# The last batch's second product in seven half-size products, and maxima that travel through DRAM

## The chip, the cores and the metric

The kernel runs on one core of one Trainium2 chip. The metric is the device time of one execution in microseconds (us). TensorE (PE) multiplies, VectorE (DVE) and ScalarE (ACT) do the elementwise work, GpSimd (POOL) almost nothing; SyncE (SP) issues nearly all DMAs, in the order of its queue.

## The reference

Sigmoid attention over 8 batches, 12 heads, 448 tokens, head size 64, and behind it two matrix products with a bend between them:

```python
scores = np.matmul(q, k.transpose(0, 1, 3, 2)) / np.sqrt(64) - np.log(448)
attn_out = np.matmul(1.0 / (1.0 + np.exp(-scores)), v)
x = attn_out.transpose(0, 2, 1, 3).reshape(8 * 448, 768)
h = x @ w_in                                # 768 x 2048
g = np.where(h >= 1, h, np.where(h <= -1, 0.0, (h + 1) ** 2 / 4.0))
out = g @ w_out                             # 2048 x 768
```

All inputs are float32.

## The kernel before

**Split operands.** From pair 8 on (a pair is two heads of one batch; 6 pairs a batch, 48 in all) every operand is scaled by a power of two and split into a high and a low float16 part, and each product of two matrices is three products (high by high, high by low, low by high). The scale comes from the largest magnitude of the operand. `prep_a` has ACT take the sums of magnitudes of q, k and v of a pair, per partition (`dump`, L597; from pair 47 on DVE takes maxima, L601). `all_sum` (L380) rounds these three columns to bfloat16 (`mb`, L383) and multiplies them by ones on PE, 128 x 3, so that every partition has the total; `total` (L664) puts this product into the score group of an earlier pair, in a spare part of its PSUM tile. `prep_b` (L604) makes the scales from it (L358 to L366, 3 columns each) and splits q, k and v (`hl`, `v`: ACT L627, DVE L628).

**A batch.** While the two big products of batch b run, the attention of batch b + 1 is spread between them: `scores` on PE, sigmoid and rounding on ACT (`psc` L736, `ahl` L744), the residue on DVE (`ahl` L745), `pav` on PE. Batch 7 has no attention of a next batch. The units of a batch are first the *ups* (x times w_in, with the bend), then the *downs* (g times w_out).

**The ups.** From batch 2 on `up_blocks` (L962) does 2 x 2 blocks in seven products instead of eight (`PRODUCTS`, L960): w_in in 8 sets i of prepared combinations, each product 128 x 128 by 224 columns, 9 of them a product, 63 an i, 504 a batch (`ph`). The sets were prepared in batch 1 by `mix` and `unmixed` and lie in DRAM (`blocks`); `load_set` brings them into three rotating slots. DVE adds the products up (L987, five of 224 columns an i; ACT L990, L996), and `bend` (L1021) does the bend on rows of 448, twice an i: ACT L1027, DVE L1028 and L1029, ACT's rounding L1030, DVE's residue L1031 into `ghl`, which holds all 16 chunks of g.

**The downs.** `down` (L1035) is plain: for 6 blocks m of rows of the output, 16 chunks by 3 products of 448 columns, 288 a batch (`po`), from `w_out_sb`, which holds all of w_out in both parts. DVE scales the result (L1064) and SP stores it. PSUM has three tiles (`ps_mo`) for `ph` and `po` together.

**The order.** `pin_order` (L282) plays the whole program with a list of costs (`Node.cost`): PE takes the first ready piece by rank, which is mostly the program's order; the other engines take, of what is ready, what is due first, where the due time comes from the PE products that need it (`play`, L226). The queues that come out are pinned. A DMA may not be placed earlier than 15 us ahead of its due time (L242).

Of the kernel before, what the change touches and what calls it, by code (L numbers as in the profile page):

```python
# [300 lines left out]
def sigmoid_attention_mlp(ctx: ExitStack, tc: tile.TileContext, first_qvk, qkv, w_in, w_out, out_t):  # L301
# [733 lines left out]
    def down(b, m, u, k):  # L1035
# [19 lines left out]
        if u == (hi - lo) // 2 - 1:  # L1055
# [8 lines left out]
                    nc.vector.tensor_scalar(out=o, in0=po[:, :S], scalar1=hold["od"], scalar2=None, op0=ALU.mult)  # L1064
# [126 lines left out]
    inv_x = finish_x(1)  # L1191
    common_scales(1, inv_x)
    mixed_at = plain_at = 0
    for b in range(1, B):
        units = ups_blocks(b) + downs(b)
        last = len(units) - 96 + LAST
        if b == 1:
# [76 lines left out]
```

## Time and profile before

| | |
|---|---|
| three runs | 1108.07, 1109.12, 1109.72 us; median 1109.12 |
| profiled execution | 1109.34 us |
| its span | 1107.6 us, 19890 instructions |
| busy | PE 1097.8, weight loads 671.8, DVE 896.6, ACT 783.8, POOL 1.3 us |
| granted clock | 1.00 |
| DMA | 151.63 MB, mean 137 GB/s |

How to read it: the span is from the first to the last instruction of one execution; the execution's own time has 1.74 us around it. In the busy lines "PEld" is PE's weight load, which overlaps products. A group row of the profile gives line, engine, operation, written tile <- read tiles, shapes and count, then busy us and mean ns of one, then the idle time of the engine just before these instructions and what ended it. A busy PE is not PE at its peak; what shows whether it was held up is what its instructions waited for.

### The profile page before, as it was taken

The numbers are of one execution on the slowest core, as the hardware profiler recorded it, in microseconds if no ns is written. First come the engines' busy times: TensorE is split into PE (matmuls) and PEld (weight loads), VectorE is DVE, ScalarE is ACT, GpSimd is POOL, SyncE is SP. The second block draws the span as 40 slices with busy tenths as digits, with TensorE's granted clock in tenths as the row PEclk, the third lists the DMA queues.
The fourth block names the chain that finished last, engine by engine and source line by source line (L and its number), as shares of the span: only waits on it lengthen the run. The fifth ranks groups of instructions, "written<-read, shape, count | busy, mean of one in ns | idle before, by whom it ended". The sixth has DMA issues, their size and how long they took to land.

```text
span 1107.6 us, 19890 instructions
## 1 busy us (share of the span) xinstructions
PE 1097.8 (99%) x7920; PEld 671.8 (61%) x7920; DVE 896.6 (81%) x1921; ACT 783.8 (71%) x1308; POOL 1.3 (0%) x8
## 2 busy tenths in 40 slices
PE   8999999999999999999999999999999999999998
PEld 2244445555447874588645885468844687459954
DVE  5999999989989997879957898679986799665820
ACT  6979998878966887568964789647886488533500
POOL 0000000000000000000000000000000000000000
PEclk9999999999999999999999999999999999999999
DMA  9924441242445605325161443416243151403400
GB/s 355 408 91 152 146 168 52 86 154 106 166 187 211 231 27 189 120 101 192 56 221 40 176 145 108 145 36 225 95 139 135 65 183 62 166 18 127 141 26 25
DMA packets 32222, 151.63 MB, mean 137 GB/s; under 512 B 3456, under 2 KB 14208, under 8 KB 25984
## 3 DMA queue, kind: packets, MB, share of 16 engines
q1 hardware_dynamic: 30400, 140.92, 35.5%
q10 hardware_dynamic: 1728, 9.44, 2.5%
q8 instruction: 62, 1.02, 0.4%
q14 instruction: 32, 0.26, 0.1%
HBM read 126.94 MB, written 23.40 MB: 136 GB/s over the span
## 4 chain that ended last, share of the span: by engine, by line
PE 90%; ACT 4%; DVE 3%; DMA 2%; issue 1%; ACTq 0%
PE po L425 38%; PE ph L425 34%; PE psc L425 10%; PE pav L425 9%; DMA w_out_sb<-w_in 1%; ACT a L733 1%; DMA blocks<-mixp 1%; DVE xhl L987 1%; DVE ahl L745 1%; ACT w_in_sb L498 1%; ACT mixp L945 0%; ACT ahl L744 0%; ACT psc L736 0%; DMA ghl<-first_qvk 0%; ACT mixs L930 0%
## 5 line engine op out<-in xcount | busy, mean ns | idle before, releaser
L425 PE MATMUL po<-ghl,w_out_sb 128*128 128x448 f16 x2304 | 445.2, 353 | 0.0
L425 PEld LDWEIGHTS <-w_in_sb 128*128 128x128 f16 x3708 | 353.2, 98 | 77.2 <-issue 18.0
L425 PEld LDWEIGHTS <-w_out_sb 128*128 128x128 f16 x2304 | 221.6, 98 | 216.6 <-issue 14.9
L425 PE MATMUL ph<-w_in_sb 128*128 128x224 f16 x3024 | 295.8, 259 | 0.3 <-DVE xhl L987 0.3
L745 DVE SCALAR_TENSOR_TENSOR ahl<-psc,ahl 128x896 f16<-128x896 f32 (+1 forms) x180 | 160.8, 901 | 63.6 <-ACT ahl L744 60.8
L736 ACT ACTIVATE psc<-psc,nls,sqk 128x896 f32<-128x896 f32 (+1 forms) x144 | 135.0, 966 | 72.4 <-PE psc L425 72.0
L744 ACT ACTIVATE ahl<-psc 128x896 f16<-128x896 f32 (+1 forms) x180 | 131.1, 760 | 9.8 <-DVE ahl L745 9.0
L425 PE MATMUL ph<-xhl,w_in_sb 128*128 128x448 f16 x576 | 111.6, 353 | 0.0
L987 DVE TENSOR_TENSOR xhl<-ph,xhl 128x224 f32<-128x224 f32 x240 | 88.9, 386 | 12.8 <-PE ph L425 7.6
L1030 ACT ACTIVATE ghl<-g 128x448 f16<-128x448 f32 x128 | 72.8, 575 | 32.8 <-DVE g L1029 32.1
L425 PE MATMUL psc<-hl 64*128 64x448 f16 (+1 forms) x744 | 85.0, 352 | 0.0
L1064 DVE TENSOR_SCALAR o<-po,od 128x448 f32<-128x448 f32 x42 | 28.6, 682 | 68.6 <-PE po L425 68.2
L1027 ACT ACTIVATE g<-xhl,hr,ihr 128x448 f32<-128x448 f32 x96 | 69.0, 756 | 21.1 <-DVE xhl L987 20.0
L1028 DVE SCALAR_TENSOR_TENSOR g<-g,rk 128x448 f32<-128x448 f32 x112 | 75.8, 681 | 7.8 <-ACT g L1027 7.3
L425 PE MATMUL pav<-ahl,v 128*64 128x448 f16 x792 | 81.8, 355 | 0.0
L1031 DVE TENSOR_TENSOR ghl<-g,ghl 128x448 f16<-128x448 f32 x128 | 77.9, 620 | 1.5
L627 ACT ACTIVATE hl<-raw,qkv_s 128x448 f16<-128x448 f32 x80 | 49.9, 664 | 24.8 <-DVE qkv_s L362 24.6
L1029 DVE SCALAR_TENSOR_TENSOR g<-xhl,ihs,g 128x448 f32<-128x448 f32 x96 | 64.9, 681 | 1.6
L597 ACT ACTIVATE dump<-raw 128x448 f16<-128x448 f32 (+1 forms) x107 | 63.5, 594 | 3.1 <-DMA raw<-qkv 1.9
L425 PEld LDWEIGHTS <-v 128*64 128x64 f16 x792 | 41.8, 110 | 37.9 <-issue 13.4
L628 DVE SCALAR_TENSOR_TENSOR hl<-raw,qkv_s,hl 128x448 f16<-128x448 f32 x80 | 52.2, 680 | 5.2 <-ACT hl L627 5.1
L425 PEld LDWEIGHTS <-hl 64*128 64x128 f16 (+1 forms) x744 | 29.5, 94 | 41.0 <-issue 19.2
(141 smaller groups left out, 898.9 us busy)
## 6 DMA issues: line engine op xcount, KB each, us to landing
w_in_sb<-blocks SPq DMA_DIRECT2D x48, 1344.0 KB, 6.1
raw<-qkv SPq DMA_DIRECT2D x36, 704.0 KB, 4.6
w_out_sb<-w_in SPq DMA_DIRECT2D x16, 768.0 KB, 11.7
out_t<-o SPq DMA_DIRECT2D x48, 224.0 KB, 2.1
blocks<-mixs SPq DMA_DIRECT2D x8, 768.0 KB, 3.8
w_out_sb<-w_out ACTq DMA_DIRECT2D x6, 768.0 KB, 5.3
raww<-w_out ACTq DMA_DIRECT2D x6, 768.0 KB, 4.5
blocks<-mixp SPq DMA_DIRECT2D x8, 576.0 KB, 4.7
```

The source lines that it names most:

```text
L425: ins = nc.tensor.matmul(*args, **kw)
L597: ins = nc.scalar.activation(dump[:, : rt.shape[1]], rt, AF.Abs, accum_out=m[:, t : t + 1])
L628: nc.vector.scalar_tensor_tensor(out=dst[:, 1, :], in0=rt, scalar=s[:, t : t + 1], in1=hi, op0=ALU.mult, op1=ALU.subtract)
L736: nc.scalar.activation(a, a, AF.Sigmoid, bias=nls, scale=sqk)
L744: nc.scalar.activation(hi, x, AF.Copy, scale=ATT)
L745: made.setdefault(i, []).append(nc.vector.scalar_tensor_tensor(out=lo, in0=x, scalar=ATT, in1=hi, op0=ALU.mult, op1=ALU.subtract))
L987: add = lambda out, q, other: nc.vector.tensor_tensor(out=out, in0=quarter(q), in1=other, op=ALU.add)
L1027: nc.scalar.activation(g, h, AF.Relu, bias=hr, scale=ihr)
L1028: nc.vector.scalar_tensor_tensor(out=g, in0=g, scalar=rt, in1=g, op0=ALU.min, op1=ALU.mult)
L1029: nc.vector.scalar_tensor_tensor(out=g, in0=h, scalar=ihs, in1=g, op0=ALU.mult, op1=ALU.max)
L1030: latest["g"] = nc.scalar.activation(hi, g, AF.Copy)
L1031: (nc.gpsimd if f % GPOOL else nc.vector).tensor_tensor(out=ghl[:, f, 1, :], in0=g, in1=hi, op=ALU.subtract)
```

## The change

**Downs of the last batch.** For batch 7 (`WB`) the plain downs give way to seven half-size products for 2 x 2 blocks, as in the ups: w_out's halves of chunks by halves of output rows, g's halves of chunks by halves of tokens. `down_blocks` does 21 turns (3 blocks m by 7 products), 8 chunks by 3 products of 224 columns each. The turns stand in the order `TURNS`: products 0 and 4 of all m, then 1, 2, 3, 6, 5 of each m; the first three turns are cut at chunk 5 (`STEPS`). ACT evicts products 0 and 4, DVE adds the others up; the last of all is one DVE addition of 224 columns and a store of 128 x 224.

**Combinations of g.** `bend_blocks` takes the place of `bend` in batch 7. Behind the same bend it makes four differences of 224 columns an i on DVE and splits seven parts instead of four: high and low of g's first halves (which products 0 and 4 need), and of the combinations (`gx`, three at a time as 672 columns, and the second half of chunk i). Its rows lie in a buffer of five (`gs`).

**Combinations of w_out.** `mix_out` and `unmixed_out`, eight of each, make the blocks and `send` stores them to DRAM (`out_blocks`, 56 stores). The program places them in batches 2 to 4, one each 13 units; their due times lie in batch 7. `load_unit` reads 21 units of 128 x 2048 into a ring of seven that lies where w_out lay: seven when the downs of batch 6 have read it, and one after each turn.

**Maxima.** From pair 20 on (`TOPS`) the three columns are written to DRAM and read back by all partitions (128 x 384, into an unused end of `w_out_sb`), both by SP, and DVE reduces them to three maxima in the scales' place; `mb` and its product are gone, 28 times.

**Planner.** A store to DRAM is no longer held to 15 us ahead of its due time.

The core of the diff:

```diff
-    ready = [x.due - 15e3 if x.dma and not x.fixed else 0.0 for x in nodes]
+    ready = [x.due - 15e3 if x.dma and not x.fixed and space(x.all[0].outs[0]) != "DRAM" else 0.0 for x in nodes]
...
             maxes[p] = m[:, :n]
+            if p >= TOPS:
+                nc.sync.dma_start(out=tops[p], in_=m)
+                nc.sync.dma_start(out=every, in_=tops[p].rearrange("k t -> (k t)").partition_broadcast(P))
...
-        m = sums.pop(p) if p in sums else alone(all_sum(m, n))
+        if p >= TOPS:
+            m = sml_p.tile([P, 3], F32, tag="m4", name="m4", bufs=1)
+            nc.vector.tensor_reduce(out=m, in_=every.rearrange("p (k t) -> p t k", t=3), axis=AX.X, op=ALU.max)
+        else:
+            m = sums.pop(p) if p in sums else alone(all_sum(m, n))
...
+    def mix_out(i):
...
+        for r, chunk in ((0, f), (1, g)):
+            nc.vector.tensor_tensor(
+                out=a[:, r], in0=w_out_sb[:, chunk, 0, :], in1=w_out_sb[:, chunk, 1, :], op=ALU.add
+            )
+        a11, a21, a12, a22 = a[:, 0, :H], a[:, 0, H:], a[:, 1, :H], a[:, 1, H:]
+        nc.vector.scalar_tensor_tensor(out=a22, in0=a21, scalar=ratio, in1=a22, op0=ALU.mult, op1=ALU.add)
+        nc.vector.tensor_tensor(out=a21, in0=a11, in1=a21, op=ALU.subtract)
+        nc.vector.scalar_tensor_tensor(out=a11, in0=a11, scalar=minus, in1=a22, op0=ALU.mult, op1=ALU.add)
+        nc.vector.tensor_tensor(out=a12, in0=a12, in1=a11, op=ALU.subtract)
...
+        for t in range(4):
+            send(i, 3 + t, sv[:, t].rearrange("p m h n -> p m (h n)"))
...
+    TURNS = [(m, j) for j in (0, 4) for m in range(HC)] + [(m, j) for m in range(HC) for j in (1, 2, 3, 6, 5)]
...
+    def bend_blocks(b, i):
...
+        parts(*(ghl[:, i + k, h, :].rearrange("p (t n) -> p t n", t=2) for h in range(2)), q[:, 2:4])
+        parts(ghl[:, i, 0, :HN], ghl[:, i, 1, :HN], q[:, 0])
+        for out, a, c in ((0, 1, 0), (1, 3, 1), (3, 3, 0), (2, 2, 3)):
+            nc.vector.tensor_tensor(out=q[:, out], in0=q[:, a], in1=q[:, c], op=ALU.subtract)
+        parts(ghl[:, i, 0, HN:], ghl[:, i, 1, HN:], q[:, 0])
+        parts(gx[:, i, :, 0], gx[:, i, :, 1], q[:, 1:4])
...
+    STEPS = [(u, 0, 5) for u in range(HC)] + [(u, 5, 8) for u in range(HC)]
+    STEPS += [(u, 0, 8) for u in range(HC, len(TURNS))]
...
+        for f in range(lo, hi):
+            for wh, gh in ((0, 0), (0, 1), (1, 0)):
+                mm(
+                    quarter(j), w[:, f, wh, :], part_of(f, gh), start=j in (0, 1, 2, 6) and f + wh + gh == 0,
+                    stop=f == k - 1 and wh == 1, skip_group_check=True,
+                )
+        if hi < k:
+            return
+        load_unit(n + NU)
...
+    turns = [60 + 13 * k for k in range(NFC)]
...
+                if b >= SB and (b - SB) * len(units) + u in turns:
+                    i = turns.index((b - SB) * len(units) + u)
+                    (mix_out, unmixed_out)[i % 2](i // 2)
```

On PE the order of products is the same up to the last batch but for the 28 that are gone and a few pieces of six `po` products that stand some pieces earlier. What moved on the other engines, at three places:

DVE at the end of the last batch's ups and behind them, before (the two L987 in one row are the last adds of the ups, for i = 7; g is the bend's row, L1031 the residue of 448):

```order
L1028 SCALAR_TENSOR_TENSOR g<-g,rk_11618 128x448
L1031 TENSOR_TENSOR ghl<-g,ghl 128x448
L1029 SCALAR_TENSOR_TENSOR g<-xhl,ihs_11622,g 128x448
L987 TENSOR_TENSOR xhl<-ph,xhl 128x224 x2
L1031 TENSOR_TENSOR ghl<-g,ghl 128x448
L1028 SCALAR_TENSOR_TENSOR g<-g,rk_11628 128x448
L1028 SCALAR_TENSOR_TENSOR g<-g,rk_11618 128x448
L1029 SCALAR_TENSOR_TENSOR g<-xhl,ihs_11632,g 128x448
L1029 SCALAR_TENSOR_TENSOR g<-xhl,ihs_11622,g 128x448
L1031 TENSOR_TENSOR ghl<-g,ghl 128x448 x2
L1064 TENSOR_SCALAR o<-po,od 128x448 x6
```

and now (L1083 are the adds, L1117 and L1118 the bend's steps, L1128 the differences, L1123 the residues; `w_out_sb` there is `gx`):

```order
L1083 TENSOR_TENSOR xhl<-ph,xhl 128x224 x2
L1128 TENSOR_TENSOR gs<-gs 128x224
L1123 TENSOR_TENSOR ghl<-gs,ghl 128x448
L1117 SCALAR_TENSOR_TENSOR g<-g,qm 128x448 x2
L1118 SCALAR_TENSOR_TENSOR gs<-xhl,ihs_11861,g 128x448 x2
L1123 TENSOR_TENSOR ghl<-gs,ghl 128x224
L1128 TENSOR_TENSOR gs<-gs 128x224
L1123 TENSOR_TENSOR ghl<-gs,ghl 128x448 x3
L1128 TENSOR_TENSOR gs<-gs 128x224 x15
L1123 TENSOR_TENSOR w_out_sb<-gs,w_out_sb 128x3x224 x5
L1123 TENSOR_TENSOR ghl<-gs,ghl 128x224 x5
L1235 SCALAR_TENSOR_TENSOR u<-po,od,u 128x224 x2
```

Seventeen differences and the combinations of five i stand behind the ups' last adds, ahead of the first sums of the downs; 15 differences, ten residues of 224 and three of 672 stand ahead of those adds, among the ups, where four residues of 448 stand now and thirteen stood before.

DVE in the downs of batch 4, between two attention pieces' residues (`ahl`), before:

```order
L793 TENSOR_REDUCE xm<-x_92 128x1 x2
L826 TENSOR_TENSOR xhl<-x_92 128x672
L383 CAST mb<-m_8063 128x3
L745 SCALAR_TENSOR_TENSOR ahl<-psc,ahl 64x448
L1064 TENSOR_SCALAR o<-po,od 128x448
L745 SCALAR_TENSOR_TENSOR ahl<-psc,ahl 128x896
L745 SCALAR_TENSOR_TENSOR ahl<-psc,ahl 64x448
L358 TENSOR_SCALAR qkv_e<-psc 128x3
```

and now:

```order
L805 TENSOR_REDUCE xm<-x_92 128x1
L1012 TENSOR_TENSOR omixa<-w_out_sb 128x768 x2
L1016 SCALAR_TENSOR_TENSOR omixa<-omixa,out_mixes 128x384
L757 SCALAR_TENSOR_TENSOR ahl<-psc,ahl 64x448
L1190 TENSOR_SCALAR o<-po,od 128x448
L757 SCALAR_TENSOR_TENSOR ahl<-psc,ahl 128x896
L757 SCALAR_TENSOR_TENSOR ahl<-psc,ahl 64x448
L619 TENSOR_REDUCE m_8277<-w_out_sb 128x3
```

The cast is gone, the reduction of 384 numbers (L619) stands ahead of the scales, and operations of `mix_out` stand between the pieces.

SP in the ups of batch 2, before (`blocks` are the sets of w_in, `raw` the pairs):

```order
L953 DMA w_in_sb<-blocks 128x5376 x2
L581 DMA raw<-qkv 128x1408
L953 DMA w_in_sb<-blocks 128x5376 x2
L1066 DMA out_t<-o 128x448
L581 DMA raw<-qkv 128x1408 x2
L1066 DMA out_t<-o 128x448
```

and now (`m` are a pair's columns):

```order
L965 DMA w_in_sb<-blocks 128x5376 x2
L609 DMA tops<-m_4027 128x3
L610 DMA w_out_sb<-tops 128x384
L609 DMA tops<-m_4381 128x3
L610 DMA w_out_sb<-tops 128x384
L586 DMA raw<-qkv 128x1408 x2
L1192 DMA out_t<-o 128x448
```

Writes and broadcasts of the maxima stand between the loads, in one queue with them.

More of the change, by code (lines that the diff above doesn't have):

```diff
@@ L54 @@
 SB = 2
+TOPS = 20
+WB = 7
 GROUPED = 8
@@ L555, in slot_of @@
         return (p + 2) % NFB
+    tops = drm_p.tile([NPAIR, P, 3], F32, name="tops")
+    every = w_out_sb.rearrange("p f h n -> p (f h n)")[:, -1024:-256].bitcast(F32)
     done = set()
@@ new lines, in block_scales, with out_scales, put @@
+        down_sc[b, None] = lambda: od
+    UNIT, NU = NFC // 2 * 2 * P, 7
+    wflat = w_out_sb.rearrange("p f h n -> p (f h n)")
+    ring = [wflat[:, k * UNIT : (k + 1) * UNIT] for k in range(NU)]
+    gx = wflat[:, NU * UNIT : NU * UNIT + NFC // 2 * 6 * HN].rearrange("p (f t h n) -> p f t h n", t=3, h=2, n=HN)
+    out_blocks = drm_p.tile([HC, 7, P, UNIT], F16, name="out_blocks")
+    out_mixed = {}
+    out_mixes = const.tile([P, 6], F32, name="out_mixes")
+    def out_scales():
+        def put(tag, in0, s1, op0, s2=None, op1=None):
+            out_mixed[tag] = t = out_mixes[:, len(out_mixed) : len(out_mixed) + 1]
+            nc.vector.tensor_scalar(out=t, in0=in0, scalar1=s1, scalar2=s2, op0=op0, **({"op1": op1} if op1 else {}))
+            return t
+        low = put("low", wo.scale[0], wo.scale[1], ALU.min, 0.25, ALU.mult)
+        put("inv", wo.inv[0], wo.inv[1], ALU.max, 4.0, ALU.mult)
+        put("to0", low, wo.inv[0], ALU.mult)
+        put("to1", low, wo.inv[1], ALU.mult)
+        put("ratio", wo.scale[1], wo.inv[0], ALU.mult)
+        put("minus", out_mixed["ratio"], -1.0, ALU.mult)
@@ new lines, in unmixed_out @@
+    def unmixed_out(i):
+        pl = raw_p.tile([P, 2 * DM], I32, tag="raww", name="omixp").bitcast(F16)[:, : 3 * DM]
+        pv = pl.rearrange("p (t m h n) -> p t m h n", t=3, m=HC, h=2)
+        for h in range(2):
+            f = w_out_sb[:, i, h, : DM // 2].rearrange("p (m n) -> p m n", m=HC)
+            nc.scalar.activation(pv[:, 0, :, h, :], f, AF.Copy, scale=out_mixed["to0"])
+            g = w_out_sb[:, i + NFC // 2, h, :].rearrange("p (t m n) -> p t m n", t=2, m=HC)
+            nc.scalar.activation(pv[:, 1:3, :, h, :], g, AF.Copy, scale=out_mixed["to1"])
+        for t in range(3):
+            send(i, t, pv[:, t].rearrange("p m h n -> p m (h n)"))
@@ L1066, in down, with down_blocks, part_of, quarter @@
             nc.sync.dma_start(out=dst, in_=o)
+    STEPS = [(u, 0, 5) for u in range(HC)] + [(u, 5, 8) for u in range(HC)]
+    STEPS += [(u, 0, 8) for u in range(HC, len(TURNS))]
+    def down_blocks(b, u, lo, hi):
+        cut()
+        m, j = TURNS[u]
+        n, k = (b - WB) * len(TURNS) + u, NFC // 2
+        if u == 0 and lo == 0:
+            hold["od"] = down_sc[b, None]()
+        if j == 0 and lo == 0:
+            hold["u", m] = tmp_p.tile([P, S], F32, tag="tmp", name="u")
+        if j in (0, 1, 2, 6) and lo == 0:
+            hold["q", m, j] = ps_mo.tile([P, 512], F32, tag="mo", name="po")
+        wt, xt, _ = PRODUCTS[j]
+        def part_of(f, gh):
+            return (
+                ghl[:, f, gh, :HN], ghl[:, f + k, gh, :HN], ghl[:, f + k, gh, HN:], ghl[:, f, gh, HN:],
+                gx[:, f, 2, gh], gx[:, f, 0, gh], gx[:, f, 1, gh],
+            )[xt]
+        home = {0: (0, 0), 4: (0, 0), 1: (1, 0), 2: (2, 0), 3: (2, 1), 5: (2, 0), 6: (6, 0)}
+        def quarter(j):
+            at, half = home[j]
+            return hold["q", m, at][:, half * 256 : half * 256 + HN]
+        w = ring[n % NU].rearrange("p (f h n) -> p f h n", f=k, h=2)
+        for f in range(lo, hi):
[3 more added lines that the diff above has]
+                    stop=f == k - 1 and wh == 1, skip_group_check=True,
+                )
+        if hi < k:
+            return
+        load_unit(n + NU)
+        od, u2, u3 = hold["od"], hold["u", m][:, :HN], hold["u", m][:, HN:]
+        def add(out, j, other):
+            nc.vector.scalar_tensor_tensor(out=out, in0=quarter(j), scalar=od, in1=other, op0=ALU.mult, op1=ALU.add)
+        def put(half, lo, hi, o):
+            row = (m + half * HC) * P
+            nc.sync.dma_start(out=out_t[row : row + P, b * S + lo : b * S + hi], in_=o)
+        if j == 0:
+            nc.scalar.activation(u2, quarter(0), AF.Copy, scale=od)
+        elif j == 4:
+            o = out_p.tile([P, S], F32, tag="o", name="o")[:, :HN]
+            nc.scalar.activation(o, quarter(4), AF.Copy, scale=od)
+            put(0, 0, HN, o)
+        elif j == 1:
+            add(u2, 1, u2)
+        elif j == 3:
+            add(u3, 2, u2)
+            hold["og"] = out_p.tile([P, S], F32, tag="o", name="o")
+            add(hold["og"][:, HN:], 3, u3)
+            put(1, HN, S, hold["og"][:, HN:])
+            add(u3, 3, u2)
+        elif j == 6:
+            o = out_p.tile([P, S], F32, tag="o", name="o")[:, :HN]
+            add(o, 6, u3)
+            put(0, HN, S, o)
+        elif j == 5:
+            add(hold["og"][:, :HN], 5, u2)
+            put(1, 0, HN, hold["og"][:, :HN])
@@ L1196, in sigmoid_attention_mlp @@
         last = len(units) - 96 + LAST
+        if b >= WB:
+            units = ups_blocks(b) + [lambda s=s: down_blocks(b, *s) for s in STEPS]
+            last = len(units) - (96 - LAST) // 2
+        if b == WB:
+            for n in range(NU):
+                load_unit(n)
+        if b == SB:
+            out_scales()
         if b == 1:
@@ L1204, in sigmoid_attention_mlp @@
         slow = [*range(n), *range(2 * n, 3 * n)] if b < SB else range(len(PRODUCTS) * NFC // 2)
-        share = [DW // 2 if u in slow else DW for u in range(last)]
+        share = [DW // 2 if u in slow else DW * (1 + (b >= WB)) for u in range(last)]
         share = [sum(share[:u]) / sum(share) for u in range(last + 1)]
```

51 lines of the change are left out of this document (48 added, 3 removed).

## The prediction

> **What bounds the kernel now.** I read the page's busy times first, then TensorE's waits, then busy times by stage, then the chain of waits in the last batch. The page:
>
> ```profile
> span 1107.6 us, 19890 instructions
> PE 1097.8 (99%) x7920; PEld 671.8 (61%) x7920; DVE 896.6 (81%) x1921; ACT 783.8 (71%) x1308; POOL 1.3 (0%) x8
> ```
>
> TensorE (PE) is busy 1097.8 of 1107.6 us. A busy matmul row could hide stalls, so here is what PE waited for; the largest and the only one on VectorE (DVE) in a batch:
>
> ```profile
> PE psc L425 <- DMA ghl<-first_qvk: 4.3, 1, 4.3
> PE ph L425 <- DVE xhl L987: 0.3, 1, 0.3
> ```
>
> So after the first load nothing makes PE wait, and the time is the sum of its products. Next, the stages (columns: PE, weight load, DVE, ACT, POOL busy, granted clock, DMA share, GB/s): one steady batch, its first half (ups) alone, and the last batch's ups and downs:
>
> ```profile
> 474.90:607.10 132.20, 132.20 (x1058) 89.13 (x1058) 108.66 (x245) 96.90 (x170) 0.00 (x0) 1.00 0.37 128
> 474.90:540.00 65.10, 65.10 (x645) 55.88 (x645) 59.41 (x127) 53.15 (x100) 0.00 (x0) 1.00 0.37 133
> 1001.20:1050.60 49.40, 49.40 (x511) 48.85 (x510) 38.63 (x80) 22.48 (x44) 0.00 (x0) 1.00 0.43 150
> 1050.60:1107.60 57.00, 53.52 (x284) 27.51 (x282) 9.08 (x15) 3.09 (x5) 0.00 (x0) 1.00 0.07 25
> ```
>
> PE has no gap at full granted clock. DVE, the fullest of the others, has 18% free over a batch, 9% in its ups and nearly everything in the last downs. A change can win by shortening PE's products, and lose where new DVE work makes PE wait.
>
> The chain that ends the kernel (start us, us, what):
>
> ```profile
> 1001.34 46.58 PE ph L425 x486
> 1047.91 1.14 PE po L425 x6
> 1049.05 1.72 PE ph L425 x18
> 1050.77 53.36 PE po L425 x282
> 1104.13 0.03 issue
> 1104.16 0.68 DVE o L1064
> ```
>
> **The change part by part.** *Products of the last down.* Before: 288 of 448 columns at 53.36 / 282 = 0.1892 us, 54.49 us. After: 21 turns of 24, so 504 of 224 columns. The ups stream exactly this size, at 46.58 / 486 = 0.0958 us: 48.30 us. Gain 6.19 us. Each of these has a weight load of 128 columns of its own, and the third window shows that stream just holding (48.85 of 49.40 us): no more is to be had.
>
> The Trainium skill, "TensorE: Matmul & The Clock Gate", section "Back-to-back issue gap", speaks against halving: for streams of weight load and matmul it gives 81 ns at 128 columns and 131 ns at 512. My estimate between these is 94 ns at 224 and 123 ns at 448, by which the down would grow from 35.3 to 47.1 us. The trace disagrees: 189 ns at 448 columns, and halves at 96.
>
> *The tail.* After the last product one DVE operation of 448 columns (0.68 us) becomes one of 224; the adds of 224 take 0.39 (rows below). Gain 0.27 us (0.39 is without a scalar operand: 0.2 to 0.3). The last store is half as large; I count nothing for it (0 to 0.3).
>
> *The maxima's products.* 28 products of 3 columns go. What one costs is read from two score groups that differ by it alone, x10 with and x9 without:
>
> ```profile
> 937.89 1.25 PE psc L425 x10
> 954.14 1.24 PE psc L425 x9
> ```
>
> 0.01 us: it lies in the change of tile shape between full and half tiles. 28 x 0.01 = 0.3 at most, by rounding perhaps 0; I take 0.14.
>
> *The last batch on DVE.* The groups of the last 106 us, and of the whole run, by mean ns:
>
> ```profile
> L987 DVE TENSOR_TENSOR xhl<-ph,xhl 128x224 f32<-128x224 f32 x40 | 14.9, 388 | 6.1 <-PE ph L425 3.0 <-ACT xhl L990 2.8
> L1028 DVE SCALAR_TENSOR_TENSOR g<-g,rk 128x448 f32<-128x448 f32 x16 | 10.9, 682 | 4.1 <-ACT g L1027 4.0
> L1031 DVE TENSOR_TENSOR ghl<-g,ghl 128x448 f16<-128x448 f32 x16 | 9.9, 622 | 0.7
> L826 DVE TENSOR_TENSOR xhl<-x 128x672 f32<-128x672 f32 x6 | 5.1, 849 | 0.0
> ```
>
> One round of i in the ups is these rows, from one L1028 with its wait to the next:
>
> ```profile
> 1028.53 0.68 DVE L1028 SCALAR_TENSOR_TENSOR g<-g,rk 128x448 f32<-128x448 f32 x1 [0.59 <-ACT g L1027]
> ...
> 1034.57 0.69 DVE L1028 SCALAR_TENSOR_TENSOR g<-g,rk 128x448 f32<-128x448 f32 x1 [0.59 <-ACT g L1027]
> ```
>
> 6.04 us, of which 0.59 idle: 5.45 us for 5 adds, 4 two-operand steps and 2 residues, whose means sum to 5.90. Neighbours overlap, so I price by 0.92 of the mean: 0.36 (224), 0.63 (step), 0.57 (448), 0.78 (672). The order of the new kernel says where the new work stands. Up to the last add of the ups it has 15 differences and 10 residues of 224, 3 residues of 672 and one step more than before, 9 residues of 448 fewer: 25 x 0.36 + 3 x 0.78 + 0.63 - 9 x 0.57 = 6.8 us. The waits of L1028 (4.0 us) are what DVE has spare; so it ends 2.8 us late. PE feels less: between the last read of a PSUM tile and the reuse of its buffer lie two products, 18 x 0.0958 = 1.7 us, less two adds (0.78) and handovers: about 0.7 us is forgiven. Stall 2.1.
>
> Then the downs. The last adds and ACT's read-out of 224:
>
> ```profile
> 1050.81 0.69 DVE L987 TENSOR_TENSOR xhl<-ph,xhl 128x224 f32<-128x224 f32 x2 [0.30 <-PE ph L425]
> L990 ACT ACTIVATE xhl<-ph 128x224 f32<-128x224 f32 x8 | 2.9, 357 | 25.1 <-PE ph L425 25.1
> ```
>
> Products 0 of the three m, cut at chunk 5, give 45 + 6 products, 4.9 us, before chunk 7 is needed. After the last add (0.7 us after the last up product) DVE has one difference, one residue, four steps, one short residue: 0.36 + 0.57 + 2.52 + 0.36 = 3.8; with 0.36 for ACT's rounding, 0.2 for handovers and the 0.7, 5.1. Stall 0.2. From there PE has 3 + 18 products, three turns 4 and seven eighths of turn (0, 1): 114 x 0.0958 = 10.9 us; DVE has 1 + 15 differences, 3 residues of 448 and 5 of 672 until the last combination is there: 16 x 0.36 + 3 x 0.57 + 5 x 0.78 = 11.4. Stall 0.5. Together 2.8 us. Ends: with differences at 0.31 the ups fit and it is 0.8; with full means about 5. Later turns find all in place; turns 0 and 4 are evicted by ACT, which had 22.48 of 49.40 us busy.
>
> *Loads of w_out blocks.* 7 units of 512 KB in the ups, 14 in the downs at one per turn of 2.3 us, each issued six turns (14 us) ahead. Rows of such transfers:
>
> ```profile
> w_in_sb<-blocks SPq DMA_DIRECT2D x48, 1344.0 KB, 6.1
> out_t<-o SPq DMA_DIRECT2D x48, 224.0 KB, 2.1
> o<-part SPq DMA_DIRECT2D x6, 224.0 KB, 2.7
> ```
>
> 1344 KB land in 6.1 us, so 512 KB in about 3: hidden behind 14. In the ups 3.7 MB join 150 GB/s x 49 us = 7.3 MB; together 224 GB/s, where the page's line of 40 slices begins with 408:
>
> ```profile
> GB/s 355 408 91 152 146 168 52 86 154 106 166 187 211 231 27 189 120 101 192 56 221 40 176 145 108 145 36 225 95 139 135 65 183 62 166 18 127 141 26 25
> ```
>
> Cost 0; if a set came late, its lateness.
>
> *Preparing the blocks (batches 2 to 6).* Eight times on DVE 2 sums of 768, 4 steps of 384, one residue of 768 and two of 384; on ACT three roundings of a mix and four copies of the unmixed parts. Rows of the like:
>
> ```profile
> L917 DVE TENSOR_TENSOR mixa<-w_in_sb 128x768 f32<-128x768 f16 x16 | 14.8, 952 | 0.0
> L922 DVE SCALAR_TENSOR_TENSOR mixa<-mixa,mixes 128x384 f32<-128x384 f32 x8 | 4.9, 618 | 0.2
> L931 DVE SCALAR_TENSOR_TENSOR mixs<-mixa,mixes,mixs 128x768 f16<-128x768 f32 x16 | 15.7, 1013 | 1.2 <-ACT mixs L930 1.2
> L930 ACT ACTIVATE mixs<-mixa,mixes 128x768 f16<-128x768 f32 x16 | 14.4, 931 | 8.8 <-DMA blocks<-mixp 6.6 <-DVE mixa L924 1.2 <-DVE mixa L922 1.0
> L793 DVE TENSOR_REDUCE xm<-x 128x1 f32<-128x448 f32 x48 | 28.8, 612 | 8.4 <-ACT x L792 7.7 <-ACT x L789 0.6
> L414 DVE TENSOR_REDUCE xm<-psc 128x1 f32<-128x128 f32 x6 | 1.7, 291 | 2.2 <-PE psc L425 2.1
> L383 DVE CAST mb<-m 128x3 bf16<-128x3 f32 (+1 forms) x40 | 6.7, 168 | 7.8 <-PE psc L425 5.8 <-ACT dump L597 1.8
> ```
>
> DVE: 2 x 0.95 + 6 x 0.62 + 1.01 = 6.6 us each. The new maximum over 384 numbers lies between 0.29 (128) and 0.61 (448): 0.55, less the cast of 0.17, 0.38 for each of 6 pairs. A batch with two mixes gains 13.2 + 2.3 = 15.5 us: 108.66 + 15.5 = 124 of 132.2, 94%. That is a little more than its ups hold today (91%) with no PE wait, and the order puts most of it into the downs. What it costs PE is not in the trace: 0 from that row, up to 5 if each of the 24 operations of about 1 us holds back a product by 0.2. I take 0.7, near the row. ACT gains at most 2 x 5 us a batch on 96.90. The planner's new rule for stores to DRAM lets them stand earlier; ACT's waits for `blocks<-mixp` in L930's row (6.6 us) may shrink, but PE did not wait for them: 0.
>
> *Maxima through DRAM.* The write and the broadcast take about 2.1 + 2.7 us plus two issues, in place of a product that waited for its score group. The two score groups above belong to neighbouring pairs, 16 us apart, and the operands of pair p + 2 are due about that much later; the reduction heads DVE's queue only where the order set it. Cost 0 in the forecast, priced as a rival.
>
> **The sum** against the profiled execution, 1109.34 us (span 1107.6 and 1.74 around it): -6.19 - 0.27 - 0.14 + 2.8 + 0.7 = -3.1, so 1106.2; the median of the runs, 1109.12, is 0.2 lower: **1106.0**.
>
> **Rivals.**
> *DVE eats the gain.* If DVE runs at full means and the mixes cost 2 us: -6.6 + 5 + 2, 1109.5: no change that can be told (0.2%, 2.2 us, is about what a measurement of this kernel tells). For it: the ups leave DVE 0.59 of 6.04 us. Against: the order keeps residues and differences behind the adds.
> *The reduction waits in DVE's queue (slower).* Behind it stand the score residues and the adds that PE needs. DVE has 132.2 - 124 = 8 us a batch left, 1.4 a pair. If the reduction waits longer than that for its broadcast, because SP is held by a load in front of it or the 1344 KB of a set (6.1 us) pass first, PE slips by the excess: at 1.7 us, 0.3 x 28 = 8.4, less the 3.1: 1114.4. For it: two hops of over 2 us where there was a product. Against: the pair of slack.
> *Halving costs.* If products from w_out went no faster than 0.108 us, 504 of them would take the old 54.5 us, and with the other terms it would be 1112. The ups' 0.0958 speak against it. The Trainium skill's rule above would put the kernel here or beyond.
> *All hidden.* No stall: 1109.1 - 6.6 = 1102.5.
>
> **Chances.** Forecast 0.60 (1102.6 to 1108), DVE eats the gain 0.18, reduction 0.11, halving 0.02, all hidden 0.09. The forecast holds a small part that rounds to no change, so: faster 0.63, same 0.23, slower 0.14. The range leaves out the reduction, halving and part of all hidden: 1102.5 to 1110.5.
>
> **What would show it.** Right: 504 products `po` of 224 columns at 0.096 us; PE waits for DVE of 2 to 4 us between the last third of the last ups and turn (0, 1), with DVE full there; elsewhere PE waits under 1.5 us; the same span of a score group without its product. Wrong: DVE idle before the reduction on a DMA by over 1 us a pair; PE waiting on `w_out_sb` from DRAM; the batches of 132.2 us growing by more than 1.

## The result, and the profile after

| | median us | lowest to highest | runs |
|---|---|---|---|
| before | 1108.62 | 1108.07 to 1109.72 | 4 |
| changed | 1119.22 | 1118.48 to 1119.67 | 4 |

The changed kernel is slower: ratio 1.0094, 95% interval 1.0076 to 1.0111. The forecast was 1106.0 us, 1102.5 to 1110.5.

The profiled execution took 1119.67 us. Its page begins:

```profile
span 1118.0 us, 20730 instructions
PE 1098.5 (98%) x8108; PEld 692.1 (62%) x8108; DVE 976.5 (87%) x2052; ACT 831.5 (74%) x1386; POOL 1.3 (0%) x8
```

PE is about as busy as before, although its products have become fewer columns, and the span is 10.4 us longer. The busy times by stage (columns as in the prediction's windows) show where. Before, batch 4 (3 and 5 have the same length), batch 6 and the last:

```profile
607.04:739.28 132.24, 132.24 (x1059) 89.17 (x1058) 108.69 (x245) 96.95 (x170) 0.00 (x0) 1.00 0.37 128
...
871.52:1001.18 129.66, 129.66 (x1036) 87.97 (x1035) 100.15 (x219) 82.01 (x135) 0.00 (x0) 1.00 0.29 102
1001.18:1107.60 106.42, 102.94 (x793) 76.38 (x791) 47.71 (x95) 25.57 (x48) 0.00 (x0) 1.00 0.23 83
```

And after, batches 4 to 7:

```profile
610.32:748.28 137.96, 134.44 (x1054) 89.73 (x1052) 123.31 (x264) 106.58 (x184) 0.00 (x0) 0.99 0.50 151
748.28:885.18 136.90, 134.22 (x1054) 89.53 (x1052) 123.52 (x264) 106.73 (x184) 0.00 (x0) 0.99 0.50 152
885.18:1016.85 131.67, 129.96 (x1032) 87.68 (x1031) 105.14 (x214) 86.06 (x141) 0.00 (x0) 1.00 0.39 125
1016.85:1118.00 101.15, 97.08 (x1009) 96.50 (x1007) 67.13 (x155) 34.33 (x70) 0.00 (x0) 1.00 0.55 189
```

Batch 4 starts 3.3 us later (610.32 against 607.04); batches 4, 5 and 6 grow by 5.7, 4.7 and 2.0, and the last takes 5.3 less: +10.4 together. So the half-size products bring most of what they were to bring, and 15.7 us are lost in the batches ahead of them. What PE waited for (us in total, times, longest):

```profile
PE ph L427 <- DVE xhl L1083: 6.3, 3, 2.5
...
PE psc L427 <- DVE ahl L757: 2.2, 2, 2.0
PE psc L427 <- DVE diag L403: 1.6, 2, 1.0
PE po L427 <- ACT ghl L1122: 0.5, 1, 0.5
```

Before, PE waited for DVE 0.5 us for `diag` (at 317.71, in batch 1, which the prediction's list leaves out) and 0.3 us for the adds. Now the adds of the ups (L1083) let PE wait 6.3 us in three places. The places in PE's timeline (start, us, instruction, idle time before it):

```profile
309.29 2.14 PE L427 MATMUL psc<-hl 64*128 64x448 f16 x12 [1.97 <-DVE ahl L757]
...
639.46 7.86 PE L427 MATMUL ph<-w_in_sb 128*128 128x224 f16 x63 [2.50 <-DVE xhl L1083]
...
776.97 7.86 PE L427 MATMUL ph<-w_in_sb 128*128 128x224 f16 x63 [2.06 <-DVE xhl L1083]
...
913.52 6.36 PE L427 MATMUL ph<-w_in_sb 128*128 128x224 f16 x63 [1.71 <-DVE xhl L1083]
```

One wait for the adds stands in the ups of each of batches 4, 5 and 6. The one at 309.29, in batch 1, is for `ahl`, and it comes before the first broadcast is issued (337.14), so no reduction that waits can be its cause. What DVE did ahead of the one at 639.46, with SP's queue beside it:

```profile
628.01 0.32 SPq L609 DMA_DIRECT2D tops<-m  x1
628.42 0.38 SPq L965 DMA_DIRECT2D w_in_sb<-blocks  x1
...
631.54 0.32 SPq L610 DMA_DIRECT2D w_out_sb<-tops  x1
...
638.16 0.66 DVE L619 TENSOR_REDUCE m<-w_out_sb 128x3 f32<-128x384 f32 x1 [3.17 <-DMA w_out_sb<-tops]
638.73 0.68 DVE L1083 TENSOR_TENSOR xhl<-ph,xhl 128x224 f32<-128x224 f32 x2
```

The write of the columns goes at 628.01, a set of 1344 KB right behind it, and the broadcast at 631.54, when the write has landed. The reduction stands at the head of DVE's queue and idles there for 3.17 us, until the broadcast is in at 638.16, 6.6 us after its issue. Behind it are two adds that PE needs, the 2.50 us above. DVE's waits of this kind over the whole run, and how long the two hops, broadcast and write, took to land (count, size, median us):

```profile
DVE m L619 <- DMA w_out_sb<-tops: 14.3, 8, 3.2
```

```profile
w_out_sb<-tops SPq DMA_DIRECT2D x28, 192.0 KB, 4.8
...
tops<-m SPq DMA_DIRECT2D x28, 1.5 KB, 4.0
```

Eight of 28 reductions found DVE waiting, 14.3 us in all, longest 3.2. The write takes 4.0 us and the broadcast 4.8 at the median, not 2.1 and 2.7.

The waits of PE are not the whole loss. The granted clock (the column ahead of the DMA share) in five us from one us behind each of the four waits above:

```profile
310.29:315.29 5.00, 5.00 (x33) 2.14 (x30) 3.73 (x9) 4.94 (x9) 0.00 (x0) 0.71 0.29 118
640.46:645.46 5.00, 5.00 (x38) 4.35 (x36) 4.39 (x8) 4.66 (x9) 0.00 (x0) 0.66 0.64 227
777.97:782.97 5.00, 5.00 (x40) 4.48 (x39) 4.39 (x8) 4.68 (x9) 0.00 (x0) 0.72 0.59 232
914.52:919.52 5.00, 5.00 (x53) 4.84 (x51) 4.83 (x10) 4.77 (x10) 0.00 (x0) 1.00 0.55 180
```

After three of the four PE ran below full clock; 5 us at 0.71, 0.66 and 0.72 cost 1.5, 1.7 and 1.4 us. That is how 63 products of one set took 7.86 us there and 6.36 behind the wait at 913.52: PE counts as busy and is slow. The waits for DVE in the rows above (6.3 + 2.2 + 1.6, 10.1 us, where before had 0.8) and the lower clock (4.6) come to 13.9 of the 15.7 us of this execution; 3.4 of them are the wait in batch 1 and the clock behind it.

The last batch's chain, from its first up product to the last addition:

```profile
1017.01 46.58 PE ph L427 x486
...
1071.17 43.49 PE po L427 x452
...
1114.69 0.45 DVE o L1235
```

The ups take 46.58 us as before, so DVE's new work there delays nothing, and the products of 224 columns run at 43.49 / 452 = 0.0962 us.

### The profile page after: what moved, and what is told of

The parts are those of the page before. It is cut to its first block, busy times and chain, and to the rows that moved or that the text cites. A ratio compares the mean times of both kernels' runs of the same rounds, so it can differ in the third digit from the quotient of the medians.

```text
span 1118.0 us, 20730 instructions
## 1 busy us (share of the span) xinstructions
PE 1098.5 (98%) x8108; PEld 692.1 (62%) x8108; DVE 976.5 (87%) x2052; ACT 831.5 (74%) x1386; POOL 1.3 (0%) x8
## 4 chain that ended last, share of the span: by engine, by line
PE 41%; DVE 29%; ACT 19%; DMA 6%; issue 5%; SPq 0%; ACTq 0%; DVEq 0%
PE po L427 20%; PE ph L427 12%; PE psc L427 5%; DVE ahl L757 5%; PE pav L427 5%; DMA w_out_sb<-tops 3%; DVE g L1154 3%; DVE xhl L1083 3%; DVE g L1155 3%; ACT dump L602 3%; ACT psc L748 2%; ACT ahl L756 2%; DVE ghl L1157 2%; ACT g L1153 2%; ACT hl L639 2%
## 5 line engine op out<-in xcount | busy, mean ns | idle before, releaser
L427 PE MATMUL po<-ghl,w_out_sb 128*128 128x448 f16 (+1 forms) x2304 | 419.2, 341 | 0.7 <-ACT ghl L1122 0.5
L427 PEld LDWEIGHTS <-w_out_sb 128*128 128x128 f16 x2520 | 241.9, 98 | 191.5 <-issue 16.0
L427 PE MATMUL ph<-w_in_sb 128*128 128x224 f16 x3024 | 299.3, 261 | 6.3 <-DVE xhl L1083 6.3
L1083 DVE TENSOR_TENSOR xhl<-ph,xhl 128x224 f32<-128x224 f32 x240 | 89.1, 386 | 11.5 <-PE ph L427 5.4
L1156 ACT ACTIVATE ghl<-g 128x448 f16<-128x448 f32 x112 | 63.2, 575 | 33.1 <-DVE g L1155 32.5
L1153 ACT ACTIVATE g<-xhl,hr,ihr 128x448 f32<-128x448 f32 x80 | 58.3, 756 | 25.4 <-DVE xhl L1083 25.0
L1154 DVE SCALAR_TENSOR_TENSOR g<-g,rk 128x448 f32<-128x448 f32 x96 | 65.0, 680 | 3.5 <-ACT g L1153 2.6
L1157 DVE TENSOR_TENSOR ghl<-g,ghl 128x448 f16<-128x448 f32 x112 | 67.4, 618 | 0.3
L427 PEld LDWEIGHTS <-v 128*64 128x64 f16 x792 | 42.1, 110 | 38.8 <-issue 14.6
L1155 DVE SCALAR_TENSOR_TENSOR g<-xhl,ihs,g 128x448 f32<-128x448 f32 x80 | 54.0, 681 | 1.4
L639 ACT ACTIVATE v<-raw,qkv_s 128x512 f16<-128x512 f32 x36 | 25.8, 717 | 27.3 <-DVE qkv_s L364 27.1
```

What stands on the lines that cost most here:

```text
L427: ins = nc.tensor.matmul(*args, **kw)
L639: nc.scalar.activation(hi, rt, AF.Copy, scale=s[:, t : t + 1])
L1083: add = lambda out, q, other: nc.vector.tensor_tensor(out=out, in0=quarter(q), in1=other, op=ALU.add)
L1153: nc.scalar.activation(g, h, AF.Relu, bias=hr, scale=ihr)
L1154: nc.vector.scalar_tensor_tensor(out=g, in0=g, scalar=rt, in1=g, op0=ALU.min, op1=ALU.mult)
L1155: nc.vector.scalar_tensor_tensor(out=g, in0=h, scalar=ihs, in1=g, op0=ALU.mult, op1=ALU.max)
```

## The experiments

Two theories stood at the start. One, *the round trip*: the reduction is set so early in DVE's queue that its broadcast has not landed, and DVE's queue behind it, then PE, pay for that. The rival, *DVE is full*: the preparation of the w_out blocks takes DVE's spare time in batches 2 to 6 and makes its adds late, whatever the maxima do. A third, smaller: the planner's new rule for stores sets the order worse.

**The maxima by a product again.** The change without its DRAM part:

```diff
-TOPS = 20
+TOPS = 48
```

> The changed kernel with the maxima by a product of ones for every pair, as before; the half-size products of the last batch, the preparation of their blocks and the planner's rule stay. Theory (the reductions wait at the head of DVE's queue for their broadcast, and PE behind them): batches 3 to 6 take 132.2 us again, the last batch keeps its 101.0 us from first up product to the end of the span; 1103 to 1106 us, the upper end if the stall of 2.0 us at 309 us stays. Rival (DVE, at 94% by the blocks' preparation, holds PE up, and the broadcasts only show it): batches 4 and 5 stay above 135 us, 1111 us or more.

Measured: 1103.11 us (1102.91 to 1103.87, 4 runs), ratio to before 0.995 (0.9936 to 0.9965). This beats both kernels. Its page's busy times, and PE's longest wait for another engine:

```profile
PE 1091.1 (99%) x8136; PEld 691.7 (63%) x8136; DVE 960.4 (87%) x2052; ACT 829.7 (75%) x1386; POOL 1.3 (0%) x8
```

```profile
PE psc L427 <- DVE diag L403: 0.9, 2, 0.7
```

DVE is as full as in the changed kernel (87%), and no add holds PE up. The rival falls; all of the loss hangs on the DRAM part, 1119.22 - 1103.11 = 16.1 us. That takes in the order that the planner makes with it: the wait in batch 1 is gone here too.

**The DRAM maxima alone**, with the plain last batch and no preparation:

```diff
-WB = 7
+WB = 8
...
-    turns = [60 + 13 * k for k in range(NFC)]
+    turns = []
```

> The maxima through DRAM from pair 20 on and the planner's rule alone: plain downs in the last batch and no blocks of w_out prepared. Theory (waits for the broadcasts): slower than before, 1113 to 1122 us, with DVE idle for w_out_sb<-tops ahead of the reductions and PE waits of about 2 us in the ups. Rival (the preparation's load on DVE): within 2 us of before, 1107 to 1111 us.

Measured: 1119.93 us (1118.48 to 1121.56, 4 runs), ratio 1.0101 (1.0086 to 1.0116). Its waits of DVE for the broadcast and of PE for the adds:

```profile
DVE m L619 <- DMA w_out_sb<-tops: 22.2, 13, 3.6
PE ph L427 <- DVE xhl L1083: 7.0, 5, 2.0
```

The waits stand in the ups again, without any of the other work: 11.1 us above the 1108.80 of before beside it. This kernel shows too that a wait need not cost clock. The place that answers to 639.46 above, and the clock behind it:

```profile
639.86 6.20 PE L427 MATMUL ph<-w_in_sb 128*128 128x224 f16 x63 [2.00 <-DVE xhl L1083]
```

```profile
640.86:645.86 5.00, 5.00 (x55) 4.94 (x52) 4.83 (x9) 2.22 (x5) 0.00 (x0) 1.00 0.53 186
```

**The planner's rule alone**: before, with only the line for stores to DRAM changed.

```diff
-    ready = [x.due - 15e3 if x.dma and not x.fixed else 0.0 for x in nodes]
+    ready = [x.due - 15e3 if x.dma and not x.fixed and space(x.all[0].outs[0]) != "DRAM" else 0.0 for x in nodes]
```

> The kernel before with the planner's new rule for stores to DRAM and nothing else. If the stall of 2.0 us at 309 us of the changed kernel, in batch 1, comes from this rule: 1110 to 1112 us, with a PE wait on DVE ahl there. If it comes from the rest of the change: 1108 to 1109 us.

Measured: 1108.02 us (1107.10 to 1109.07, 10 runs), ratio 0.9993 (0.9984 to 1.0003). The rule costs nothing in the kernel before, which has no `tops` and no `out_blocks` to store.

**The preparation alone**: w_out's blocks are made and stored, the last batch stays plain, the maxima come by a product.

```diff
-TOPS = 20
-WB = 7
+TOPS = 48
+WB = 8
```

> The blocks of w_out are prepared and stored, as in the change, but not used: plain downs in the last batch, maxima by products. What the preparation costs by itself: the prediction took 0.7 us (0 to 5) from a DVE at 94% in batches 3 to 5. Theory (filling work costs nothing): 1107.5 to 1109.5 us, batches of 132.2 us. Rival (a DVE that full holds PE up): 1110 us or more, batches above 132.7.

Measured: 1108.64 us (1107.66 to 1109.49, 10 runs), ratio 0.9995 (0.9986 to 1.0005). The 16 groups of operations on DVE, ACT and SP cost PE nothing that can be measured.

**The planner told how long the hops take.** The changed kernel; the planner counts 4 us more for both transfers, for what must come before them and for what comes after. Nothing else is edited, so only the order moves.

```diff
-            x.due -= LATE[x.engine] + x.cost_ns + 2500 * x.dma
+            x.due -= LATE[x.engine] + x.cost_ns + 2500 * x.dma + 4000 * any("tops" in q[0] for _, q in x.touched)
...
-            end = wire + 1700
+            end = wire + 1700 + 4000 * any("tops" in q[0] for _, q in x.touched)
```

> The changed kernel, its planner counting 4 us more for each of the two transfers of the maxima, both in their due times and in when they land, so that the order sets the reductions later; nothing that is computed changes. Theory (the order sets the reductions too early for what the transfers take): DVE waits for w_out_sb<-tops under 3 us in all, 14.3 before; 1104 to 1109 us. Rival (two hops can't be hidden at all, or DVE's load): over 1113 us.

Measured: 1107.97 us (1106.89 to 1109.41, 10 runs), ratio 0.9993 (0.9983 to 1.0002). DVE's waits for the broadcast, and a broadcast and reduction in the same stretch as above:

```profile
DVE m L619 <- DMA w_out_sb<-tops: 1.7, 1, 1.7
```

```profile
637.11 0.61 SPq L610 DMA_DIRECT2D w_out_sb<-tops  x1
...
651.70 0.67 DVE L619 TENSOR_REDUCE m<-w_out_sb 128x3 f32<-128x384 f32 x1
```

The hops still land in 3.6 and 4.8 us, but the reduction now stands 14.6 us behind its broadcast and waits for nothing. Eleven of the 16 us come back by the order alone. What is left against the kernel without DRAM maxima is 4.9 us; PE waits there for `ahl` (1.9, 0.9 and 0.7 us, the first and the last in batch 1) and `diag` (1.4, where the kernel without DRAM maxima has 0.9), no longer for the adds.

**A queue of their own.** Why do the hops take so long: because they stand in SP's queue among the sets, or because all transfers share the DMA engines? First both by GpSimd:

```diff
-                nc.sync.dma_start(out=tops[p], in_=m)
-                nc.sync.dma_start(out=every, in_=tops[p].rearrange("k t -> (k t)").partition_broadcast(P))
+                nc.gpsimd.dma_start(out=tops[p], in_=m)
+                nc.gpsimd.dma_start(out=every, in_=tops[p].rearrange("k t -> (k t)").partition_broadcast(P))
```

> The changed kernel with both transfers of the maxima issued by GpSimd on its own queue, not by SP behind the loads of sets and pairs; the planner's costs as in the change. Theory A (the transfers are late because they stand behind 1344 and 704 KB loads in SP's queue): tops<-m and w_out_sb<-tops land in about 2 to 3 us each, DVE waits for them under 4 us in all, 1103 to 1107 us. Theory B (two hops take that long in any queue, for the 16 DMA engines are shared): they land in 4 to 5 us as before and it stays at 1114 us or more.

Measured: 1152.29 us (1148.75 to 1155.46, 4 runs), ratio 1.0397 (1.038 to 1.0415). Landing, and waits:

```profile
w_out_sb<-tops POOLq DMA_DIRECT2D x28, 192.0 KB, 4.7
tops<-m POOLq DMA_DIRECT2D x28, 1.5 KB, 5.5
```

```profile
DVE m L619 <- DMA w_out_sb<-tops: 40.8, 11, 8.2
```

The hops are no shorter, and the waits are longer: PE waits 19.1 us for the adds in three places and 14.1 for `ahl` in twelve. GpSimd does not hold the broadcasts back there. In all eleven places where a reduction waited, the broadcast was issued 0.6 to 0.7 us behind the landing of its write; by SP it was under 0.1 us in the place shown above. It is the landings that come late. Ahead of the longest wait (8.2 us, in the same stretch as above) the write took 7.0 us and the broadcast 7.1:

```profile
630.76 0.54 POOL L609 DMA_DIRECT2D tops<-m  x1 [51.74 <-ACT dump L602]
...
638.48 0.55 POOL L610 DMA_DIRECT2D w_out_sb<-tops  x1 [7.17 <-DMA tops<-m]
```

Then the write alone by ACT's queue, the broadcast by SP as before:

```diff
-                nc.sync.dma_start(out=tops[p], in_=m)
+                nc.scalar.dma_start(out=tops[p], in_=m)
```

> The changed kernel, with the write of the three columns (the first hop) issued by ACT's queue and the broadcast still by SP. It tells apart what makes the hops land in 4.0 and 4.8 us (medians of the changed kernel). Theory A, the queue: on SP the write stands behind, or is followed by, a set of 1344 KB and passes with it; on a queue of its own the first hop lands in about the 2 us of its shortest, the reduction's waits of 14.3 us in all (8 of them) fall to under 8, and PE's waits for DVE's adds of the ups fall below 3 us in all: about 1112. Theory B, the shared DMA engines: the first hop still lands in 3.5 to 5 us whatever the queue, since the sets and the attention's loads move at the same time; PE's waits stay between 5 and 12 us, and the time stays within 5 us of the changed kernel: 1115 to 1124. The write now also holds ACT's queue until DVE or ACT has the columns; if ACT waits there for its own sums alone, nothing is added. The broadcast by SP needs the write landed, so it can hold what stands behind it on SP; that is as before.

Measured: 1125.72 us (1124.36 to 1126.53, 4 runs), ratio 1.0148 (1.0131 to 1.0165). Landing, and DVE's waits:

```profile
tops<-m ACTq DMA_DIRECT2D x28, 1.5 KB, 4.4
```

```profile
DVE m L619 <- DMA w_out_sb<-tops: 17.4, 8, 4.4
```

The queue is not the cause of the landing times: 1.5 KB take 4.4 us on ACT's queue too. The time is 1.7 us above the range of the theory of shared engines: PE waits 9.8 us for the adds in three places, where it waited 6.3. The stretch in which the broadcast of the changed kernel was under way moves 303 GB/s, with the DMA engines 84% busy; a write that landed in 2.2 us found them idle (0.03):

```profile
631.54:638.16 6.62, 5.42 (x52) 4.33 (x50) 3.45 (x7) 4.38 (x8) 0.00 (x0) 1.00 0.84 303
...
680.18:682.38 2.20, 2.20 (x16) 0.82 (x15) 2.12 (x5) 1.25 (x3) 0.00 (x0) 1.00 0.03 1
```

This holds for all the writes. In the changed kernel ten of the 28 landed in 2.0 to 2.9 us, and the DMA engines were 8% busy on average between issue and landing; the other 18 took 3.5 to 7.1 us at 69%. By ACT's queue it was 11 writes under 3 us at 10% and 17 over it at 68%, by GpSimd's 8 at 9% and 20 at 70%. So the landing time goes with what else the DMA engines carry, in every queue; no run took that load away by itself.

The Trainium skill, "DMA: Bandwidth & Descriptors", section "Issuing engines are not separate DMA queues", says that transfers of all issuing engines run on the same 16 DMA engines and interleave. The landing times of SP, GpSimd and ACT, 4.0, 5.5 and 4.4 us for the same 1.5 KB, agree in that no queue of its own is faster.

**The order of the turns.** The kernel without DRAM maxima, with the 21 turns block by block and no cut at chunk 5:

```diff
-    TURNS = [(m, j) for j in (0, 4) for m in range(HC)] + [(m, j) for m in range(HC) for j in (1, 2, 3, 6, 5)]
+    TURNS = [(m, j) for m in range(HC) for j in (0, 4, 1, 2, 3, 6, 5)]
...
-    STEPS = [(u, 0, 5) for u in range(HC)] + [(u, 5, 8) for u in range(HC)]
-    STEPS += [(u, 0, 8) for u in range(HC, len(TURNS))]
+    STEPS = [(u, 0, 8) for u in range(len(TURNS))]
```

> The kernel of e1_no_dram_maxima with the 21 turns of the last downs in plain order: 0, 4, 1, 2, 3, 6, 5 of each block m, none cut in two. If DVE's combinations of g are hidden by the order of the turns, as the prediction had it: turn 1 of the first block comes four turns (9 us) earlier and PE waits there for w_out_sb from DVE, 7 to 9 us in all; 1110 to 1112 us. If the last batch's DVE work fits under the ups anyway: within 1.5 us of e1_no_dram_maxima, 1103 to 1105 us.

Measured: 1113.10 us (1111.89 to 1113.42, 5 runs), ratio 1.0033 (1.002 to 1.0047), 10.0 us above the same kernel with the written order. PE's waits in the last batch, and a window behind the second of them:

```profile
PE po L427 <- DVE w_out_sb L1123: 1.8, 4, 0.9
PE po L427 <- ACT ghl L1122: 1.8, 1, 1.8
PE po L427 <- ACT u L1241: 1.3, 1, 1.3
```

```profile
1054.70:1057.70 3.00, 3.00 (x17) 2.45 (x17) 3.00 (x9) 0.00 (x0) 0.00 (x0) 0.50 0.46 152
```

The work behind the bend is no longer covered: 4.9 us of waits where the written order has 0.7, and behind them PE at half clock (PE counts 1097.1 us busy against 1091.1). Both ranges were missed. The theory had 7 to 9 us of waits for DVE's combinations and at most 1112 us; they took 1.8, the rest are waits for ACT's rounding of g (1.8) and its read-out (1.3), and the theory had not counted the lower clock, which costs about as much as the waits. So the cover that the written order gives is needed; the run does not part the order of the turns from the cut at chunk 5.

**No sharing of the maxima.** From pair 20 on each partition scales by its own columns; there is no product, no transfer and no reduction. The sharing across partitions is left out.

```diff
-            if p >= TOPS:
-                nc.sync.dma_start(out=tops[p], in_=m)
-                nc.sync.dma_start(out=every, in_=tops[p].rearrange("k t -> (k t)").partition_broadcast(P))
...
-            m = sml_p.tile([P, 3], F32, tag="m4", name="m4", bufs=1)
-            nc.vector.tensor_reduce(out=m, in_=every.rearrange("p (k t) -> p t k", t=3), axis=AX.X, op=ALU.max)
+            pass
```

> The changed kernel from pair 20 on without any sharing of the maxima: each partition scales by its own three columns (so that part of the computation is left out), with no product, no transfer and no reduction. Against e1_no_dram_maxima, which differs by the 28 products, casts and their waits, it says what their removal could bring at most. The prediction took 0.14 us (0 to 0.3): 1102.5 to 1103.5. If the products held score groups or scales back: 1100 to 1102.

Measured: 1105.50 us (1105.20 to 1106.49, 6 runs), ratio 0.9968 (0.9956 to 0.998). This is outside both ranges: 2.4 us above the kernel in which the product shares them (2.0 by the two ratios). 1.1 us of it stands ahead of batch 2, where PE waits 1.18 us for `ahl`. So taking the 28 products away wins nothing here, even with nothing in their place; as the planner's order changes with it, the run does not tell what a product costs by itself.

## Why the prediction was wrong

The step that failed is the one on the maxima through DRAM: "Cost 0 in the forecast, priced as a rival". Its two supports both gave way. *The hops*: I took 2.1 + 2.7 us from stores of `o` and loads of `part`; they took 4.0 + 4.8 at the median and 3.5 + 6.6 in the place shown. The rows that I took are medians, and they hide a wide spread: single stores of `o` took 1.9 to 7.8 us in the trace of before. The three places where PE was reached are in the ups, when sets of 1344 KB move. *The slack*: that the operands of a pair are due 16 us later says when they are needed, not where the reduction stands. I wrote that it "heads DVE's queue only where the order set it", and the order did set it there: the planner lets a transfer land 1.7 us behind its last byte, which for an idle wire is 2.8 us behind the issue of the write and 3.3 behind that of the broadcast, allows 2.5 us in its due time, and takes of what it believes ready whatever is due first. The run with 4 us more in both shows it: 14.3 us of DVE's waits become 1.7, and 1119.22 becomes 1107.97.

The rival named the mechanism, DVE's queue held by a reduction ahead of PE's adds, "because SP is held by a load in front of it or the 1344 KB of a set (6.1 us) pass first". Its price of 8.4 us was too small, and its form was wrong. It spread 1.7 us over every pair against a mean slack of 1.4; in fact 20 of 28 reductions waited for nothing and eight for 14.3 us, and once in each of batches 4, 5 and 6 PE was reached through the adds. A mean slack says nothing of a wait that comes in one piece. For the same reason one sign named for it stayed out, DVE idle by over 1 us a pair (14.3 / 28 is 0.5), while another came: batches that grow by more than 1 us. Part of the loss is no wait of this kind at all: the stop in batch 1 and the lower clock.

The other terms:

- *Products of the last down*, -6.19: at 0.0962 us for 504, 48.5 us against 54.49, -6.0. Right.
- *The tail*, -0.27: 0.45 against 0.68, -0.23. Right.
- *The 28 products*, -0.14: too small to be told; the run without sharing, whose order differs too, gained nothing.
- *Stalls of the last batch*, +2.8: 0.7 (0.5 and 0.2, both ahead of chunk 7, where I had 0.2); none in the ups and none at turn (0, 1). The place of 2.1 us was wrong, in part by the price of DVE's operations. I took 0.92 of a mean; where they stand dense, they follow each other faster, as DVE's timeline behind the last ups shows:

```profile
1073.07 4.62 DVE L1128 TENSOR_TENSOR gs<-gs 128x224 f32<-128x224 f32 x15
1077.60 3.93 DVE L1123 TENSOR_TENSOR w_out_sb<-gs,w_out_sb 128x672 f16<-128x672 f32 x5
```

  0.31 us for a difference where I had 0.36, and 0.79 for 672 as priced. For the 25 of 224 in the ups that is 1.3 us of the 2.8 us that I had DVE late by. It was not late at all. The bend's first step, whose waits of 4.0 us I had taken as what DVE has spare, still waits 0.5 us, so the new work used up 3.5 us there and not 6.8:

```profile
L1117 DVE SCALAR_TENSOR_TENSOR g<-g,qm 128x448 f32<-128x448 f32 x16 | 10.8, 678 | 0.5 <-ACT g L1116 0.5
```

  Of this difference of 3.3 us the price explains 1.3; the rest stays open. The prediction's low end, 0.8 us ("with differences at 0.31 the ups fit"), is what came. The 0.7 us that PE forgives DVE held elsewhere: DVE's waits of 3.17, 2.63 and 2.29 us for broadcasts became 2.50, 2.06 and 1.71 of PE's.
- *Preparing the blocks*, +0.7: 0 (0.9995, interval 0.9986 to 1.0005). *Loads of w_out blocks*, 0: no wait of PE for them. Right, though they landed in 4.8 us at the median, not in about 3.

Without the maxima the sum would have been 1106.0 against 1103.11 measured, 2.9 too high, 2.1 of it the last batch's stalls and 0.7 the preparation. The halving itself, and the row of 0.0958 us that it rested on, were read rightly; the halving rival and the DVE rival are out.

Still open: the lower clock after some of PE's waits was seen and not tried by itself, and so is why the changed kernel loses 16.1 us to the DRAM maxima where they alone cost 11.1. The three stretches of lower clock (4.6 us) are of that size, and the kernel with the maxima alone ran at a mean granted clock of 1.000, the changed one at 0.995. But the other three executions of the changed kernel had 0.998, which is some 3 us more of full clock, and were only 0.4 to 1.2 us shorter; so the clock is not shown to be the whole of it. Nor was it tried why PE waits for `ahl` in batch 1 in kernels without the 28 products (1.97 us in the changed one, 1.25 with the maxima alone, 1.18 without sharing) and not where they are kept; the order that the planner makes differs from there on.

## What to carry to other kernels

A transfer that takes the place of a product is not priced by its landing time alone: ask at whose head the instruction that reads it stands, and what the scheduler believes of its landing. An in-order engine with work that others need behind a wait for a transfer passes on what is longer than their slack (here all but 0.6 to 0.7 us); set the reader later than the worst landing under load, not the median of quiet ones. And an edit that bundles two ideas is best run apart: here one half gains 5.7 us, and the other loses 11 alone and 16 beside it.

## What the hardware showed

*Half clock after short waits.* One-us windows behind the wait that ended at 639.46 (the windows ahead of and behind these are at 1.00):

```profile
640.46:641.46 1.00, 1.00 (x10) 0.89 (x8) 1.00 (x2) 0.97 (x3) 0.00 (x0) 0.68 0.91 297
641.46:642.46 1.00, 1.00 (x8) 0.79 (x7) 0.93 (x3) 1.00 (x3) 0.00 (x0) 0.50 0.94 361
...
643.46:644.46 1.00, 1.00 (x8) 0.85 (x7) 0.97 (x3) 1.00 (x3) 0.00 (x0) 0.61 0.39 151
```

The clock falls to 0.50 over a us after PE has started again; behind the waits at 309.29 and 776.97 it falls within the first us (0.72 and 0.69 in it). The four us, the one not shown at 0.50 too, miss 0.32 + 0.50 + 0.50 + 0.39 = 1.7 us of full clock, which is 3.4 us at half. Waits of 1.97, 2.06 and 2.50 us were followed by such a stretch here; 1.71 us here, 2.00 in the kernel with the maxima alone and 2.37 and 2.49 in the one with GpSimd's queue were not. In the kernel with the turns by block a wait of 1.78 us with one of 1.31 close behind it was enough, and later four shorter ones (1.8 us in all). All seven waits of 3.0 us or more behind the first load, in the runs with GpSimd's and ACT's queues, had PE at 0.50 at once. So the chance grows with the wait, and no single length parts the two. The Trainium skill, "TensorE: Matmul & The Clock Gate", section "HAM oscillation — how this bites in real kernels", gives as its rule that PE should have no idle gap above about 3.4 us. The gap does not agree: about 2.0 us was enough here, and 2.49 was not each time. Its half clock is what the windows show.

*Small transfers under load.* 1.5 KB took between 2.0 and 7.1 us to land by SP, under 3 us with the DMA engines 8% busy and 3.5 us or more at 69%, and a queue of its own did not shorten the median (4.0 by SP, 4.4 by ACT, 5.5 by GpSimd).
